# Layer 0's first product of feature tiles 8 to 15 for two token chunks together in seven block products, with a new order of the first part

## The chip, the core and the metric

The kernel runs on one core of a Trainium2 chip. Its engines are TensorE (in the rows PE for matmuls, PEld for weight loads), VectorE (DVE), ScalarE (ACT), GpSimd (POOL) and SyncE (SP, which here only issues DMAs). The metric is the device time of one execution in microseconds (us); smaller is better. All times below come from the runs and from one profiled execution of the kernel before.

## What is computed

The reference is a block attention over 1536 tokens (2 x 768, 8 heads of 64), followed by two feed-forward layers of width 2048:

```python
x = attention(q, k, v)                       # [1536, 512]
h = x @ w_in;  g = s * max(h, 0)**2 + b;  x = g @ w_out      # layer 0
h = x @ w_in2; g = max(0.01 * h, h);      out = g @ w_out2   # layer 1
```

Everything is float32. w_in is 512 x 2048, w_out 2048 x 512, in both layers.

## The kernel before

**Tiling.** The tokens go in three chunks of 512 (in the code c = 0, 1, 2; here chunk 1, 2, 3), the 2048 features in 16 feature tiles of 128 (fc). A step i is one layer, one chunk and one feature tile, in the order of the list `steps`: 0 to 15 are layer 0 of chunk 1, 16 to 31 of chunk 2, 32 to 47 of chunk 3, and 48 to 63 layer 1 of chunk 1.

**A plain step.** Each float32 operand is split into a high and a low part (hi is a rounded copy on ScalarE, lo the difference), and three matmuls (hi x hi, lo x hi, hi x lo) make one product. So the *first product* of a step (`ffn_in`) is 4 x 3 = 12 matmuls of 128x128 by 512 columns into a PSUM bank h, and the *second product* (`ffn_out`) is 4 x 3 = 12 more into the four accumulators acc. Between them stand the activation (`ffn_relu`, `ffn_act`), the split of its result g (`ffn_hi` on ScalarE, `ffn_lo` on VectorE), and the splits of the two weight blocks, tiles win and wout (`split_hi` on ScalarE, `split_lo` on GpSimd or VectorE).

**Weights.** They come from DRAM as float64 in tiles st and are turned into float32 tiles w, half a feature tile at a time, by `rescale` (ScalarE), `low_bits` (VectorE or GpSimd) and `shift` (VectorE). This is called a conversion here; each layer has 32.

**Layer 1 of chunks 2 and 3** is done with the Strassen-Winograd scheme: both chunks, two feature tiles and the two halves of the 512 inputs make a 2 x 2 block product, done in seven block products (`block`, 6 matmuls each) where eight would be 48 matmuls. Forms, which are sums and differences of blocks, are made of the tokens (`token_forms`: t1 to t4, split into hi and lo) and of the weights (`weight_forms`: s1 to s4, GpSimd); `split_block` splits the seven weight operands and `after_block` adds the products up on VectorE. A group of seven products is a quad. The second product of chunk 2 runs between them; chunk 3's activations wait and its second products come at the end (`last_chunk`), one step per 12 matmuls.

**Order.** Engines take their instructions in program order. The first part (attention of 24 units, all of layer 0 of chunk 1, and layer 0 of chunk 2) is written out in the string HEAD, a list of short operation names with numbers: s, x, e, r, n, t, c, o are the stages of an attention unit (scores, maximum, exponential, reciprocal, normalising, transpose, copy out of PSUM, output product), y and Y the hi and lo of its result, L, R, u/up, B the load and conversion of weights, H and lp/lv the weight splits, I the first and O the second product, A, a/as, G, g the activation and its split. `ops` maps each name to a call. After HEAD (from step 33) a loop goes on, one step after the other. Chunk 3's tokens come from units 16 to 23. Before, HEAD spreads these over the layer-0 steps of chunk 2.

**Slots.** Two PSUM banks h and four acc, two `at`; two tiles each of win, wout and g; two tiles vt, that hold the attention's v.

Of the kernel before, what the change touches and what calls it, by code (L numbers as in the profile page):

```python
# [25 lines left out]
P = 128  # L26
# [77 lines left out]
def block_attention_moe_moe(ctx, tc, q, k, v, vn, w1, w2, mask, ident_in, pool_in, out):  # L104
# [397 lines left out]
    def x_hi(c, m):  # L502
        if c:
# [3 lines left out]
            nc.scalar.activation(out=xf[c][m], in_=accs[0, c][m], func=AF.Copy, scale=sign)  # L507
# [27 lines left out]
    tf, wform, wops, banks, late_g = {}, {}, {}, {}, {}  # L535
# [6 lines left out]

    def token_forms(cc, part):

        if "t1" not in tf:
            for name in ("t1", "t2"):
                t = att.tile([P, GU, DM], F32, name="vt").bitcast(F32R).rearrange("p (a c) n -> p a c n", a=2)
                tf[name] = [[t[:, a, m, :] for m in range(2)] for a in range(2)]
            four = [soft.pool.tile([P, 512], F32, name=f"sm{i}").bitcast(F32R) for i in range(4)]
            tf["t4"] = [four[:2], four[2:]]  # L550
            for name, c, k in (("b11", 1, 0), ("b21", 1, 2), ("t3", 2, 0), ("b22", 2, 2)):
                tf[name] = [[xt[c][:, a, k + m, :] for m in range(2)] for a in range(2)]
# [21 lines left out]
    def open_forms():  # L574
        for i in range(2):
# [3 lines left out]
    def open_blocks():  # L579
        wops["tiles"] = [wspl.tile([P, 2, 512], F32R, name="win") for _ in range(2)]  # L580
# [342 lines left out]
```

## Time and profile before

| | us |
|---|---|
| median of 3 runs | 587.88 (587.74 to 588.04) |
| the profiled execution | 587.98 |
| its span, first to last instruction | 586.2 |
| PE busy in the span | 571.5 (98%) |
| DVE, ACT, POOL busy | 348.5, 343.5, 232.2 |

The profiled execution's own time is 1.8 us longer than the span of its trace, and 0.10 us above the median. A timeline row gives the start and the duration of an instruction; successive matmuls overlap, so the pace is read from start to start. A window row gives, for each engine, how long it was busy in a stretch.

### The profile page before, as it was taken

How to read it: one execution, taken by the hardware profiler on the slowest of the kernel's cores; microseconds unless marked ns; L12 is line 12 of the kernel's file. 1: busy time of each engine (PE TensorE's matmuls, PEld its weight loads, DVE VectorE, ACT ScalarE, POOL GpSimd, SP SyncE). 2: the span in 40 equal slices, each digit the busy share in tenths (PEclk: the TensorE clock that was granted, in tenths of full speed). 3: DMA queues.
4: the chain of work that ended last, by engine and by line, in shares of the span. 5: the costliest groups of instructions: out<-in, count | busy, mean ns of one | idle time of the engine just before them, and what ended most of it. 6: DMA issues, size and time to landing. Idle time of an engine off the chain costs nothing.

```text
span 586.2 us, 8857 instructions
## 1 busy us (share of the span) xinstructions
PE 571.5 (98%) x3196; PEld 459.5 (78%) x3196; DVE 348.5 (59%) x706; ACT 343.5 (59%) x757; POOL 232.2 (40%) x269
## 2 busy tenths in 40 slices
PE   4999999999999999999999999999999999999997
PEld 3477777878787788888888888888888888888885
DVE  5878778674523353376676678985254444446543
ACT  4788867666855563665655756655454455545342
POOL 4554555424244132333422255564455555550000
PEclk9999999999999999999999999999999999999999
DMA  8977666470400000013342433320010000000102
GB/s 340 377 224 242 215 237 210 151 244 2 162 0 1 2 1 1 1 37 107 108 129 88 144 107 101 115 73 1 1 72 1 0 2 1 1 0 9 65 1 72
DMA packets 16307, 53.38 MB, mean 91 GB/s; under 512 B 2024, under 2 KB 2408, under 8 KB 15624
## 3 DMA queue, kind: packets, MB, share of 16 engines
q1 hardware_dynamic: 16040, 52.69, 26.7%
q8 instruction: 25, 0.41, 0.3%
q14 instruction: 18, 0.15, 0.1%
q10 hardware_dynamic: 224, 0.13, 0.1%
HBM read 49.08 MB, written 3.15 MB: 89 GB/s over the span
## 4 chain that ended last, share of the span: by engine, by line
PE 93%; DVE 3%; DMA 1%; ACT 1%; issue 1%; POOL 1%; SPq 0%; POOLq 0%; DVEq 0%; ACTq 0%
PE h L446 30%; PE acc L496 22%; PE acc L498 15%; PE at L618 7%; PE h L618 7%; PE at L498 4%; PE h L498 4%; PE at L338 2%; PE at L258 2%; PE at L357 2%; DMA w<-in_q 1%; PE acc L258 1%; PE h L357 1%; ACT w L301 1%; DVE win L437 0%
## 5 line engine op out<-in xcount | busy, mean ns | idle before, releaser
L446 PE MATMUL h<-xt,win 128*128 128x512 f32 x768 | 188.7, 391 | 0.5 <-DVE win L437 0.5
L446 PEld LDWEIGHTS h<-xt,win 128*128 128x128 f32 x768 | 143.0, 188 | 32.0 <-DVE win L437 0.9
L496 PE MATMUL acc<-g,wout 128*128 128x512 f32 x576 | 145.4, 394 | 0.1
L496 PEld LDWEIGHTS acc<-g,wout 128*128 128x128 f32 x576 | 106.4, 188 | 23.4 <-issue 1.3
L437 POOL TENSOR_TENSOR win<-w,win 128x512 fp32r<-128x512 f32 x47 | 66.7, 1422 | 92.6 <-ACT win L431 67.8
L498 PE MATMUL acc<-wout,g 128*128 128x512 f32 x384 | 98.8, 390 | 0.0
L437 DVE TENSOR_TENSOR wout<-w,wout 128x512 fp32r<-128x512 f32 x74 | 70.4, 952 | 40.3 <-ACT wout L431 40.0
L431 ACT CAST wout<-w 128x512 fp32r<-128x512 f32 x96 | 59.6, 621 | 53.8 <-PE acc L496 24.4
L498 PEld LDWEIGHTS acc<-wout,g 128*128 128x128 f32 x384 | 72.1, 188 | 15.4
L479 DVE SCALAR_TENSOR_TENSOR g<-h,own,g 128x512 fp32r<-128x512 f32 x48 | 35.8, 746 | 40.1 <-ACT g L472 40.1
L417 DVE SCALAR_TENSOR_TENSOR w<-st,w 128x512 int32<-128x512 int32 x64 | 47.6, 745 | 9.8 <-ACT st L397 6.3
L457 ACT ACTIVATE r<-h 128x512 f32<-128x512 f32 x48 | 28.6, 596 | 36.1 <-PE h L446 36.1
L437 POOL TENSOR_TENSOR wout<-w,wout 128x512 fp32r<-128x512 f32 x22 | 28.9, 1315 | 51.5 <-ACT wout L431 51.3
L472 ACT ACTIVATE g<-h,own 128x512 fp32r<-128x512 f32 x48 | 32.9, 686 | 26.5 <-DVE h L467 13.2
L431 ACT CAST win<-w 128x512 fp32r<-128x512 f32 x64 | 39.3, 615 | 8.6 <-PE h L446 8.6
L483 DVE TENSOR_TENSOR g<-r,g 128x512 fp32r<-128x512 f32 x32 | 22.9, 714 | 34.9 <-ACT g L474 34.8
L397 ACT ACTIVATE st<-st 128x512 f32<-128x512 f32 x64 | 42.5, 675 | 1.1 <-DMA st<-in_w 1.1
L467 DVE TENSOR_TENSOR h<-r,h 128x512 f32<-128x512 f32 x30 | 20.8, 694 | 36.4 <-ACT r L457 36.1
L608 POOL TENSOR_TENSOR win<-q,win 128x256 fp32r<-128x256 f32 x32 | 25.7, 803 | 28.1 <-ACT win L607 28.1
L627 ACT ACTIVATE r<-r 128x512 f32<-128x512 f32 x16 | 10.1, 632 | 38.0 <-DVE r L648 19.9
L608 POOL TENSOR_TENSOR win<-w,win 128x256 fp32r<-128x256 f32 x24 | 19.9, 831 | 29.5 <-ACT win L607 17.2
L498 PE MATMUL h<-wout,g 128*128 128x512 f32 x96 | 26.9, 389 | 0.0
(149 smaller groups left out, 766.4 us busy)
## 6 DMA issues: line engine op xcount, KB each, us to landing
st<-in_w SPq DMA_DIRECT2D x64, 512.0 KB
vt<-in_v SPq DMA_DIRECT2D x5, 1024.0 KB
kt<-in_k SPq DMA_DIRECT2D x8, 500.0 KB
out<-kt SPq DMA_DIRECT2D x11, 256.0 KB
q<-in_q SPq DMA_DIRECT2D x8, 256.0 KB
w<-in_vn SPq DMA_DIRECT2D x3, 512.0 KB
w<-in_q SPq DMA_DIRECT2D x4, 256.0 KB
w<-in_v SPq DMA_DIRECT2D x2, 512.0 KB
```

What stands on the lines that cost most here:

```text
L397: nc.scalar.activation(out=high, in_=high, func=AF.Prelu, scale=2.0**-112, alpha=2.0**32)
L417: nc.vector.scalar_tensor_tensor(out=f, in0=high, scalar=3, in1=f, op0=ALU.logical_shift_left, op1=ALU.bitwise_or)
L431: nc.scalar.copy(t[:, 0, :], wf[layer, fc][:, half, :])
L437: engine.tensor_sub(t[:, 1, :], wf[layer, fc][:, half, :], t[:, 0, :])
L446: nc.tensor.matmul(hs[i], lhsT=w[:, a, cc * P : (cc + 1) * P], rhs=xt[c][:, b, cc, :], start=(cc == 0 and a == b == 0), stop=(cc == NCC - ...
L457: nc.scalar.activation(out=rs[i], in_=hs[i], func=AF.Relu)
L472: nc.scalar.activation(out=gs[i][:, 0, :], in_=hs[i], func=AF.Identity, bias=shift_b, scale=1.0)
L479: nc.vector.scalar_tensor_tensor(out=g[:, 1, :], in0=hs.pop(i), scalar=shift_b, in1=g[:, 0, :], op0=ALU.add, op1=ALU.subtract)
L496: nc.tensor.matmul(acc[m], lhsT=w[:, a, ms], rhs=g[:, b, :], start=first, stop=last)
L498: nc.tensor.matmul(acc[m], lhsT=g[:, b, ms], rhs=w[:, a, :], start=first, stop=last)
L608: nc.gpsimd.tensor_sub(t[:, 1, :], src, t[:, 0, :])
L618: nc.tensor.matmul(banks[j, name], lhsT=t[:, a, cc * P : (cc + 1) * P], rhs=x[b][cc], start=(cc == a == b == 0), stop=(cc == b == 1),)
```

## The change

Chunks 2 and 3 now take layer 0's feature tiles 8 to 15 together, in four quads of seven block products (`quads(0, NS // 2, 0)`, NS = 8). Feature tiles 0 to 7 of both chunks stay plain steps. For this the tokens of chunk 3 are needed before chunk 2's feature tile 8, so HEAD now ends with step 23, after all 24 attention units. The token forms are made at the end of HEAD from the split tokens xt (`first_forms`, operations ta on VectorE, tap on GpSimd; `first_hi`, th; `first_lo`, tl on GpSimd, tlv on VectorE); F and E are the weight forms and the first three weight splits. Chunk 3's activations of tiles 8 to 15 are kept where the weight tile was (`late_g`), and their second products come after chunk 3's plain steps, one step per 12 matmuls (`late_split`). Layer 1's weight conversions move: 11 halves stand in chunk 3's part, the other 21 in the first twelve steps of layer 1 of chunk 1, where 1.75 a step stand instead of about one, and they stand behind the split of g. HEAD is a new list throughout.

```diff
 HEAD = '''
-k0 km0 kpv0 sb k2 q0 mask sl0 sp0 iden km2 kpv2 q1 k1 s1 x0 e0 q2 s4 own d0 s5 rb0 v0 v1 x1 r0 e1 km1 x5 n0 kp1 e5 rb1
...
+k1 d0 zero k0 km0 d0 mask kpv0 km1 q0 sb s1 kpv1 sl0 x1 own sp0 e1 pool x0 d0 iden rb1 e0 k2 km2 q2 rb0 d0 kpv2 r1 r0
...
+    def first_forms(x, sub, add):
+        cc, k = divmod(x, 4)
...
+        if k == 0:
+            sub(a, h12, h11)
+            add(a, a, l12)
+            sub(a, a, l11)
+        elif k == 1:
+            sub(b, h22, a)
+            add(b, b, l22)
+        elif k == 2:
+            sub(c, h21, b)
+            add(c, c, l21)
+        else:
+            sub(d, h22, h12)
+            add(d, d, l22)
+            sub(d, d, l12)
...
+    def add_act(layer, r, x, ps):
+        if layer:
+            nc.vector.tensor_add(r, x, ps)
+            nc.scalar.activation(out=r, in_=r, func=AF.Prelu, scale=1.0, alpha=0.01)
+        else:
+            nc.vector.tensor_add(ps, x, ps)
+            nc.scalar.activation(out=r, in_=ps, func=AF.Relu)
+            nc.vector.tensor_mul(r, r, ps)
...
+    def quads(layer, first, begun):
+        for j in range(first, NQ):
+            for p in range(len(PRODUCTS)):
+                if j > first or p >= begun:
+                    block(layer, j, p)
...
+                after_block(layer, j, p, first)
+                if j > first or p:
+                    emit_out(1 + (p == len(PRODUCTS) - 1))
...
+    def late_split(layer, fc):
+        i = (3 * layer + 2) * NFC + fc
+        (hs, rs)[layer][i] = late_g(layer, fc)
         split_hi(i, 1)
         split_lo(i, 1, nc.vector)
         ffn_hi(i)
...
+    quads(0, NS // 2, 0)
...
+        convert((at + 1) * left // 12 - at * left // 12)
```

The end of HEAD, on TensorE. Before, this is where the last attention units stand, between plain steps 30 to 33 (L357 the output products of units, L338 transposes, L446 first and L496 second products, xt_97 and xt_98 the tokens of chunks 2 and 3):

```order
L338 MATMUL at_2565<-ident,sm_2488 120x128 x4
L338 MATMUL at_2572<-ident,sm_2535 120x128 x4
L496 MATMUL acc<-g,wout 128x512 x3
L446 MATMUL h<-xt_97,win 128x512 x6
L496 MATMUL acc<-g,wout 128x512 x6
L357 MATMUL at_2603<-sm_2570,vt 64x64 x8
L357 MATMUL at_2616<-sm_2577,vt 64x64 x8
L496 MATMUL acc<-g,wout 128x512 x3
L446 MATMUL h<-xt_97,win 128x512 x12
L496 MATMUL acc<-g,wout 128x512 x15
L446 MATMUL h<-xt_98,win 128x512 x12
```

Now the output products of units 22 and 23 (L353, the second and third row) stand ahead of the first products of steps 22 and 23 (L442), and the block products (L665) follow; vt is token form t2, at_ and h are banks:

```order
L334 MATMUL at_2283<-ident,sm_2275 120x128 x4
L492 MATMUL acc<-g,wout 128x512 x3
L353 MATMUL at_2302<-sm_2223,vt 64x64 x8
L353 MATMUL at_2325<-sm_2290,vt 64x64 x8
L442 MATMUL h<-xt_97,win 128x512 x12
L492 MATMUL acc<-g,wout 128x512 x12
L442 MATMUL h<-xt_97,win 128x512 x12
L492 MATMUL acc<-g,wout 128x512 x24
L665 MATMUL h<-xt_97,win 128x512 x6
L665 MATMUL at_2471<-vt,win 128x512 x6
L492 MATMUL acc<-g,wout 128x512 x3
L665 MATMUL h<-xt_97,win 128x512 x6
```

The attention now ends before feature tile 8 of chunk 2, and right behind the second products of the plain steps stand the block products, of which the second reads a form.

VectorE at the same place. Before, behind units 22 and 23 it goes on with plain steps (L374 the low parts of the units' tokens, L467 the activation, L479 the low part of g, L437 weight splits):

```order
L369 CAST xt2_98<-at1_2616 128x256
L437 TENSOR_TENSOR wout_2648<-w_1431,wout_2648 128x512
L374 TENSOR_TENSOR xt2_98<-at1_2616,xt2_98 128x256
L479 SCALAR_TENSOR_TENSOR g_2654<-h_2555,own_94,g_2654 128x512
L467 TENSOR_TENSOR h_2630<-r_2668,h_2630 128x512
L374 TENSOR_TENSOR xt2_98<-at0_2603,xt2_98 128x256
L437 TENSOR_TENSOR wout_2697<-w_1602,wout_2697 128x512
L479 SCALAR_TENSOR_TENSOR g_2700<-h_2630,own_94,g_2700 128x512
L437 TENSOR_TENSOR win_2704<-w_663,win_2704 128x512
L479 SCALAR_TENSOR_TENSOR g_2729<-h_2674,own_94,g_2729 128x512
```

Now the forms stand there. kt_2017 and kt_2018 are forms (L570 to L578), L598 are their low parts, of which the last row is that of t2's second half; L370, L475 and L433 are the tokens' low part, g's and the weight split:

```order
L370 TENSOR_TENSOR xt2_98<-at1_2302,xt2_98 128x256
L475 SCALAR_TENSOR_TENSOR g_2396<-h_2340,own_94,g_2396 128x512
L570 TENSOR_TENSOR kt_2017<-xt2_98,kt_2017 128x512
L571 TENSOR_TENSOR kt_2017<-kt_2017,xt2_98 128x512
L576 TENSOR_TENSOR kt_2018<-xt2_98 128x512
L577 TENSOR_TENSOR kt_2018<-kt_2018,xt2_98 128x512
L578 TENSOR_TENSOR kt_2018<-kt_2018,xt2_98 128x512
L598 TENSOR_TENSOR vt_2314<-kt_2017,vt_2314 128x512
L433 TENSOR_TENSOR wout_2412<-w_904,wout_2412 128x512
L598 TENSOR_TENSOR sm1_2427<-kt_2018,sm2_2358 128x512
L475 SCALAR_TENSOR_TENSOR g_2416<-h_2378,own_94,g_2416 128x512
L598 TENSOR_TENSOR vt_2315<-kt_2017,vt_2315 128x512
```

The forms of the last units' tokens and their low parts moved in between the splits of the last plain steps; ahead of this stretch stand nine more rows from the weight split of step 21, wout_2311, on.

VectorE in layer 1 of chunk 1, one step. Before (L437 the split of wout, L407 and L417 a conversion, L483 the low part of g, L562 a token form):

```order
L437 TENSOR_TENSOR wout<-w,wout 128x512
L407 TENSOR_SCALAR w<-st 128x512
L417 SCALAR_TENSOR_TENSOR w<-st,w 128x512
L483 TENSOR_TENSOR g<-r,g 128x512
L562 TENSOR_TENSOR kt<-kt 128x512
```

Now (L433, L479, L403, L413 and L616 are the same operations):

```order
L433 TENSOR_TENSOR wout<-w,wout 128x512
L479 TENSOR_TENSOR g<-r,g 128x512
L403 TENSOR_SCALAR w<-st 128x512
L413 SCALAR_TENSOR_TENSOR w<-st,w 128x512
L403 TENSOR_SCALAR w<-st 128x512
L413 SCALAR_TENSOR_TENSOR w<-st,w 128x512
L616 TENSOR_TENSOR kt<-kt 128x512
```

The conversions moved behind the low part of g, and most steps have two.

## Rows read from the trace of the kernel before

**Rows 1.** The page: PE's busy time and the clock that TensorE was granted.
```profile
PE 571.5 (98%) x3196; PEld 459.5 (78%) x3196; DVE 348.5 (59%) x706; ACT 343.5 (59%) x757; POOL 232.2 (40%) x269
PEclk9999999999999999999999999999999999999999
```

**Rows 2.** The chain that ended last, by line, as shares of the span.
```profile
by line: PE h L446 29.6%; PE acc L496 21.6%; PE acc L498 14.9%; PE at L618 6.6%; PE h L618 6.6%; PE at L498 3.7%; PE h L498 3.7%; PE at L338 1.7%; PE at L258 1.6%; PE at L357 1.5%; DMA w<-in_q 0.8%; PE acc L258 0.8%; issue 0.7%; PE h L357 0
```

**Rows 3.** Windows: stretch, its length, busy us (and count) of PE, PEld, DVE, ACT, POOL, clock, DMA.
```profile
0.00:15.00 15.00, 6.58 (x104) 5.22 (x104) 8.03 (x44) 6.04 (x25) 6.65 (x29) 1.00 0.88 340
15.00:60.00 45.00, 43.59 (x449) 29.93 (x449) 36.11 (x128) 37.56 (x112) 23.59 (x35) 1.00 0.82 284
60.00:105.00 45.00, 44.43 (x305) 34.58 (x304) 35.49 (x85) 33.49 (x89) 23.20 (x28) 1.00 0.62 210
105.00:240.00 135.00, 135.00 (x847) 108.29 (x846) 65.87 (x174) 80.43 (x186) 45.45 (x45) 1.00 0.17 59
420.00:540.00 120.00, 120.00 (x524) 98.08 (x523) 59.15 (x92) 60.60 (x128) 60.39 (x78) 1.00 0.03 9
540.00:570.00 30.00, 30.00 (x134) 24.82 (x133) 15.57 (x25) 13.20 (x24) 0.00 (x0) 1.00 0.10 36
```

**Rows 4.** PE's timeline in a plain step of layer 1: start, duration, line, tiles, count.
```profile
376.09 2.88 PE L446 MATMUL h<-xt,win 128*128 128x512 f32 x12
378.81 2.88 PE L498 MATMUL acc<-wout,g 128*128 128x512 f32 x12
```

**Rows 5.** PE's timeline: the output products of the last four attention units.
```profile
229.34 1.15 PE L357 MATMUL at<-sm,vt 120*64 120x64 f32 x32
```

**Rows 6.** Windows with one line alone, up to there: L446, then L496.
```profile
0.00:230.50 230.50, 93.34 (x372) 68.73 (x372) 1.00 0.44 153
...
0.00:230.50 230.50, 89.09 (x343) 62.67 (x343) 1.00 0.44 153
```

**Rows 7.** VectorE's timeline in one of these steps.
```profile
377.27 1.77 DVE L437 TENSOR_TENSOR wout<-w,wout 128x512 fp32r<-128x512 f32 x1
378.96 0.41 DVE L407 TENSOR_SCALAR w<-st 128x512 int32<-128x512 int32 x1
379.48 0.69 DVE L417 SCALAR_TENSOR_TENSOR w<-st,w 128x512 int32<-128x512 int32 x1
380.30 0.69 DVE L483 TENSOR_TENSOR g<-r,g 128x512 fp32r<-128x512 f32 x1
380.91 1.79 DVE L562 TENSOR_TENSOR kt<-kt 128x512 f32<-128x512 f32 x1
382.62 1.78 DVE L437 TENSOR_TENSOR wout<-w,wout 128x512 fp32r<-128x512 f32 x1
```

**Rows 8.** GpSimd's timeline at the same time.
```profile
380.86 1.29 POOL L572 TENSOR_TENSOR xt<-kt,xt 128x512 fp32r<-128x512 f32 x1 [2.37 <-ACT xt L571]
382.11 1.74 POOL L437 TENSOR_TENSOR win<-w,win 128x512 fp32r<-128x512 f32 x1
```

**Rows 9.** VectorE's timeline in a late second product of layer 1, where GpSimd is idle.
```profile
547.29 0.69 DVE L437 TENSOR_TENSOR wout<-w,wout 128x512 fp32r<-128x512 f32 x1 [1.43 <-ACT wout L431]
547.90 0.69 DVE L483 TENSOR_TENSOR g<-xt,g 128x512 fp32r<-128x512 f32 x1
```

**Rows 10.** GpSimd's timeline in a quad: one split of a weight operand, one form.
```profile
447.80 0.74 POOL L608 TENSOR_TENSOR win<-q,win 128x256 fp32r<-128x256 f32 x1
...
453.00 0.74 POOL L597 TENSOR_TENSOR q<-q,w 128x256 f32<-128x256 f32 x1
```

**Rows 11.** What PE waited for, us in total, times, longest.
```profile
PE acc L258 <- DMA w<-in_q: 7.7, 2, 6.4
PE acc L258 <- DVE kt L171: 0.8, 1, 0.8
...
PE h L446 <- DVE win L437: 0.5, 1, 0.5
```

**Rows 12.** DMA issues: the mask's queue, packets and size.
```profile
msk<-in_mask SPq DMA_DIRECT2D x1, 180.0 KB
```

More of the change, by code (lines that the diff above doesn't have):

```diff
@@ L541, in bank, with late_t4 @@
         return ps_at.pool.tile([P, 512], F32, name=f"at{n // 2}") if n % 2 else ps_h.tile([P, 512], F32, name="h")
-    def token_forms(cc, part):
[L545 to L552, printed above, removed]
+    def late_t4(layer, i):
+        tf["t4"][i // 2][i % 2] = soft.tile(("t4", layer, i)).bitcast(F32R)
@@ L604, in split_block @@
             return
-        src = weight_block(j, PRODUCTS[p])
+        if wops.get("of") != layer:
+            wops["of"], wops["tiles"] = layer, [wspl.tile([P, 2, 512], F32R, name="win") for _ in range(2)]
+        src = weight_block(layer, j, PRODUCTS[p])
         t = wops["tiles"][n % 4 // 2][:, :, n % 2 * 256 : n % 2 * 256 + 256]
@@ L788, in block_attention_moe_moe, with load_next, convert, chain @@
-    assert not late
+    todo = [(n_ffn1 + fc, half) for fc in range(NFC) for half in range(2)]
+    ahead = list(todo)
+    def load_next(n):
+        for _ in range(min(n, len(ahead))):
+            load_w(*ahead.pop(0), nc.sync)
+    def convert(n, engine=nc.vector):
+        now = [todo.pop(0) for _ in range(min(n, len(todo)))]
+        for w in now:
+            rescale(*w)
+        for w in now:
+            low_bits(*w, engine)
+            shift(*w)
+        load_next(len(now))
+    def chain(i):
+        ffn_relu(i)
+        ffn_act(i)
+        ffn_hi(i)
+        ffn_lo(i)
@@ new lines, in first_in @@
+    def first_in(i):
+        for part in range(2):
+            ffn_in(i, part)
+    c1, c2 = NFC, 2 * NFC
+    queue = [("out", c1 + NS - 1, m) for m in range(4)]
+    load_next(3)
+    quads(0, NS // 2, 0)
+    for n in range(4):
+        soft.free(("t4", 0, n))
+    split_hi(c2 + 1, 0)
+    split_lo(c2 + 1, 0, nc.gpsimd)
+    split_hi(c2, 1)
+    split_lo(c2, 1, nc.vector)
+    first_in(c2)
+    chain(c2)
+    emit_out(len(queue))
+    for m in range(4):
+        x_hi(1, m)
+    for k in range(NS):
+        i = c2 + k
+        if k + 1 < NS:
+            first_in(i + 1)
+        else:
+            for m in range(4):
+                ffn_out(c2 + NS, m)
+        if k + 2 < NS:
+            split_hi(i + 2, 0)
+            split_lo(i + 2, 0, nc.gpsimd)
+        if k + 1 < NS:
+            split_hi(i + 1, 1)
+            split_lo(i + 1, 1, nc.vector)
+        else:
+            late_split(0, NS + 1)
+        if k + 1 < NS:
+            chain(i + 1)
+        if k + 4 == NS:
+            t = att.tile([P, GU, DM], F32, name="vt").bitcast(F32R)
+            j = c2 + NS
+            ws[1][j], gs[j], hs[j] = t[:, :2, :], t[:, 2:, :], late_g(0, NS)
+            nc.scalar.copy(ws[1][j][:, 0, :], wf[0, NS][:, 1, :])
+            split_lo(j, 1, nc.vector)
+            nc.scalar.activation(out=gs[j][:, 0, :], in_=hs[j], func=AF.Identity, bias=shift_b, scale=1.0)
+            ffn_lo(j)
+        if k > 1:
+            convert(1, nc.gpsimd)
+        if k % 2:
+            split_x([[xt[1][:, a, m, :] for m in range(4)] for a in range(2)], k // 2, xf[1][k // 2])
+        for m in range(4):
+            ffn_out(i, m)
@@ new lines, in block_attention_moe_moe @@
+    for fc in range(NS + 1, NFC):
+        if fc + 1 < NFC:
+            late_split(0, fc + 1)
+        elif fc + 1 == NFC:
+            split_hi(n_ffn1, 1)
+            split_lo(n_ffn1, 1, nc.vector)
+        convert(int(fc > NS + 2), nc.gpsimd)
+        if fc + 3 >= NFC and fc + 1 < NFC:
+            at = n_ffn1 + fc + 3 - NFC
+            split_hi(at, 0)
+            split_lo(at, 0, nc.gpsimd)
+        if fc + 1 == NFC:
+            first_in(n_ffn1)
+            chain(n_ffn1)
+        for m in range(4):
+            ffn_out(c2 + fc, m)
@@ L802, in block_attention_moe_moe @@
         elif i + 2 == nq:
[L803 to L805 removed]
+            for n in range(LEAD):
+                split_block(1, n)
         if i + 1 < nq:
```

259 lines of the change are left out of this document (126 added, 133 removed).

## The prediction

> **What bounds the kernel now.** I read the page's busy line first: TensorE is busy 571.5 of 586.2 us at the full granted clock from end to end [rows 1]. The chain of waits, by line, then shows that nearly all of its share is TensorE's matmuls [rows 2]. The windows tell where the rest is: from 0 to 15 us TensorE works 6.6, in 15 to 60 it is idle 1.4, in 60 to 105 0.6, and from 105 on it has no idle time at all [rows 3]. What TensorE waits for is mostly the first q, 7.7 us in two waits [rows 11]. So TensorE's matmul count is the bound; a matmul taken away is worth its full price as long as no other queue becomes late.
>
> **Removed matmuls.** Twelve plain matmuls take 2.72 from start to start, 0.2267 each [rows 4]. The 336 matmuls of the eight quads of layer 1 (L618) hold 6.6% + 6.6% of 586.2 us in the chain [rows 2], 0.2303 each. Layer 0's eight feature tiles of two chunks were 16 × 12 = 192 plain matmuls, 43.5 us; now they are 4 × 42 = 168 block matmuls, 38.7 us. That gives −4.8.
>
> **The attention in less time.** HEAD now ends with step 23, and all 24 attention units must be done by then. Before, the last output products start at 229.34 [rows 5], and up to 230.5 TensorE ran 372 matmuls of first and 343 of second products [rows 6]: 715 × 0.2267 = 162.1 us, so 68.4 us went to attention and idle time. Now 504 product matmuls stand there, 114.3 us: the last unit comes at about 182.7. The mixture as dense as in 60 to 105 must therefore last to 183, 78 us longer. In that window VectorE is busy 35.5 and ScalarE 33.5 of 45, and TensorE is idle 0.57 [rows 3], so 78 us cost 78/45 × 0.57 = 1.0. The worse bound is the rate of 15 to 60, where VectorE is busy 36.1 and ScalarE 37.6 [rows 3]: 78/45 × 1.41 = 2.4. The other bound is nothing. For the forms' 24 new instructions on VectorE, 0.61 each from start to start [rows 9], there is room: it was busy 65.9 of 135 in 105 to 240 [rows 3]; without some 48 us of plain steps (two splits, a conversion, an activation, about 3 us per 5.44) that is 39.5, with the forms 54 of 78, 70%. I take +1.0, since the busy shares lie nearer to those of 60 to 105.
>
> **The joint between HEAD and the quads.** The second block product reads t2, whose last low part hangs on the last attention units. Behind their output products TensorE has 60 product matmuls, 6 of the first block product and 5 of the second that need no late part: 71 × 0.2267 = 16.1 us. VectorE has, from the weight split wout_2311 to that low part (vt_2315), 21 instructions; at 0.61 [rows 9] that is 12.8, a margin of 3.3. Two things eat it. GpSimd works beside it on three weight operands of 0.74 each [rows 10] and one split (wout_2394) of 1.29 [rows 8], 3.5 together. The VectorE form at 380.91 takes 1.79 while GpSimd runs, and the GpSimd instruction in the same time 1.74 where the one before took 1.29 [rows 7, 8]; with GpSimd idle the same size takes VectorE 0.69 [rows 9]. So each GpSimd instruction can cost VectorE up to its whole length; half, 1.75, is what I take. And g of step 22 stands on ScalarE behind a weight's high part whose tile step 20's second products free; no row shows that wait; it lies between 0 and one step's 2.72, I take 1.0. That leaves 0.5 of margin. The third block product's weight operand stands behind token low and high parts on GpSimd and ScalarE, by one instruction or none: 0 to 0.6. Bounds for the joint: 0, and 3.5 + 2.7 − 3.3 = 2.9. With the mean at the edge I take +0.5.
>
> On that contention the Trainium skill has a rule (page "SBUF — State Buffer", section "Who interferes with whom"): a VectorE instruction with two SBUF inputs and a GpSimd instruction that reads SBUF share a port pair, and whoever issues first has it for the whole instruction, while the other is fully blocked. The trace agrees: 1.79 against 0.69 [rows 7, 9]. By that rule with every meeting lost, the joint would be at its upper bound; by it with VectorE first every time, at zero.
>
> **Layer 1, chunk 1.** Layer 0's quads run without conversions, so 21 of layer 1's 32 now stand in its first twelve steps, 1.75 a step, behind the low part of g. VectorE takes per step, from start to start [rows 7, 9]: the split of wout 1.69, a conversion half 0.52 + 0.61 = 1.13, the low part 0.61, a form 1.71. A step with one half and a form is 5.14, with two 6.27, with two and no form 4.56; TensorE's step is 2 × 2.72 = 5.44 [rows 4]. In the pattern of 1, 2, 2, 2 halves, with forms in the steps where they stand, the end of the low part, counted from TensorE's start of the step, moves each step by the difference to 5.44: 4.8 in the first, 7.8 in the eighth, 8.3 at most, in the tenth. The second products begin to need it at 3 × 2.72 + 0.45 = 8.6, the fourth block of 2.72 and two matmuls on. Margin 0.3. Nothing is lost if these durations hold, but the shift (0.69) was seen there with GpSimd idle [rows 7, 8]. If each of 21 halves took 0.18 more, the loss would be 21 × 0.18 − 0.3 = 3.5. I take +0.2, bounds 0 and 3.5.
>
> **The late second products** of layer 0 are nine steps of 2.72 in which VectorE has two splits, 1.2 [rows 9], and in most a conversion's shift. As the late steps of layer 1 leave VectorE busy 15.6 of 30 and ScalarE 13.2 [rows 3], a shift of 0.61 more per 2.72 fits. Nothing. The kept g of the late tiles costs no copy that TensorE waits for.
>
> **The start.** SP now issues the mask ahead of the first q: 180 KB [rows 12] at the 340 GB/s of the first window [rows 3] are 0.5 us ahead of the load that TensorE waits for [rows 11]. Against it, k lands in another order, and the wait of 0.8 for VectorE's kt [rows 11] may go. +0.2, bounds −0.7 and +0.5.
>
> **Sum.** −4.8 + 1.0 + 0.5 + 0.2 + 0.2 = −2.9, against the profiled execution's 587.98: 585.1. That execution lies 0.10 above the median, so 585.0.
>
> **Rivals.**
>
> A, the forecast: 585.0, by the sum.
>
> B, no new wait: the dense stretch and all queues hold. −4.8 and nothing else, 583.1. For it speaks that VectorE and GpSimd lived side by side, busy 59 and 60 of 120 us, in 420 to 540 without a single idle slice of TensorE [rows 3]; against it the margins of 0.5 and 0.3.
>
> C, VectorE becomes the bound in layer 1: its mean load in the twelve steps is 1.69 + 0.61 + 1.75 × 1.13 + 8/12 × 1.71 = 5.4, just TensorE's 5.44. With 0.18 more per half 3.5 are lost: 585.0 − 0.2 + 3.5 = 588.3, no measurable change. It decides from 0.02 more per half on. Against it: the conversions stand behind the low part, so they delay only what follows.
>
> D, slower: VectorE comes late to the joint because GpSimd blocks it. Just before, GpSimd has three forms and two splits at 1.29 [rows 8], four weight forms at 0.74 [rows 10] and about 1 us of normalising, 10.4 us. If VectorE's instructions lose half of each, they arrive L = 5.2 late. At the joint all four GpSimd instructions (3.5) and 1.0 on ScalarE then use up 3.3 and 1.2 more, and 0.6 for the third operand follows: the stall is 1.2 + 0.6 + 5.2 = 7.0, in place of 0.5. That is 591.5, slower. It ends beyond 0.2% from L = 2.8 on. The Trainium skill's rule of the shared ports (same page and section) is what would make D. Against it: VectorE has about 30% free in that stretch and would have to lose that first.
>
> E, the denser HEAD loses as much as 15 to 60 does: 2.4 in place of 1.0, 586.4, with a few tenths at the units' waits on either side of the bound of 0.2%.
>
> That the change does not do what it says is not open: the order has 24 matmuls fewer.
>
> **How the numbers follow.** A 0.44, B 0.18, C 0.14, E 0.07, D 0.17. A measurement of this kernel can tell about 0.2%, 1.2 us, from no change: faster is below 586.70, slower above 589.06. Faster is A, B and a third of E, 0.64; within 0.2% C and the rest of E, 0.19; slower D, 0.17. Predicted is A, 585.0. The range must leave out no more than 0.2: D alone is left out. Below it reaches to B with the better start, 583.1 − 0.7 = 582.4, above to C with 0.9 at the joint, 589.2.
>
> **What would show it.** In the changed kernel's trace: 3172 matmuls where 3196 were [rows 1], and a block product of layer 0 in about 1.38; the last unit's output products near 183, and TensorE idle in 105 to 183 about 1.0 (E: over 2). At the joint, about 16 us behind them, a wait of TensorE on VectorE's vt_2315 of 0 to 1 (D: 5 and more, with VectorE's forms at 1.3 to 1.8 each and GpSimd busy in the same slices). In layer 1 of chunk 1 no wait for g (C: waits for VectorE's low part from the eighth step on, and shifts longer than 0.69). In the nine late steps 2.72 each. The first q should land about half a microsecond later. The sum is wrong if TensorE's idle time grows by more than 4.8, or if the block matmuls of layer 0 take longer than 0.2303, since their operands are then late.

## The result

The changed kernel takes 583.4 us (583.15 to 583.63), the kernel before 587.96 in the same comparison; the ratio is 0.9916, interval 0.9904 to 0.9929. It is faster by 4.6 us. The forecast was 585.0, inside a range of 582.4 to 589.2: direction right, size 1.6 short, and nearer to rival B (583.1) than to A. The profiled span went from 586.2 to 581.8.

The page after, in its busy line (engine, busy us, share, instructions) and the granted clock in 40 slices:

```profile
PE 566.5 (97%) x3172; PEld 455.1 (78%) x3172; DVE 388.2 (67%) x762; ACT 342.2 (59%) x771; POOL 257.9 (44%) x310
PEclk9999999999999999999999999999999999999999
```

Against [rows 1], 24 matmuls are gone, TensorE's busy time is 5.0 less and VectorE's 39.7 more. The clock stays at the upper level.

Windows of the changed kernel (stretch, length, busy us and count of PE, PEld, DVE, ACT, POOL, clock, DMA); the first is to be read beside [rows 3]:

```profile
60.00:105.00 45.00, 45.00 (x299) 36.16 (x298) 34.97 (x84) 31.86 (x74) 26.43 (x31) 1.00 0.74 236
105.00:183.00 78.00, 78.00 (x609) 61.30 (x608) 58.45 (x167) 54.52 (x153) 32.47 (x39) 1.00 0.26 87
...
330.00:420.00 90.00, 89.31 (x391) 72.95 (x390) 72.50 (x83) 54.21 (x99) 47.65 (x39) 1.00 0.32 100
```

The kernel before, in the last of these stretches:

```profile
330.00:420.00 90.00, 90.00 (x399) 74.45 (x398) 65.99 (x74) 54.72 (x98) 44.07 (x34) 1.00 0.25 77
```

In the 78 us in which the attention now runs dense, TensorE is never idle. Idle time has come in a place where the kernel before had none, between 330 and 420, layer 1 of chunk 1. What TensorE waited for, in the changed kernel (us in total, times, longest):

```profile
PE acc L254 <- DVE kt L167: 7.1, 1, 7.1
PE acc L254 <- DVE kt L171: 2.3, 1, 2.3
...
```

The rest of the list is 0.6 for a q at 21.5 us and, in layer 1 of chunk 1 (L494), 0.4 and 0.2 for VectorE. The start waits for k where it waited for q [rows 11]. From 22 us on, over the joint and up to layer 1, no wait is listed.

### The profile page after: what moved, and what is told of

It is laid out like the page before. It is cut to its first block, busy times and chain, and to the rows that moved or that the text cites. A ratio compares the mean times of both kernels' runs of the same rounds, so it can differ in the third digit from the quotient of the medians.

```text
span 581.8 us, 8967 instructions
## 1 busy us (share of the span) xinstructions
PE 566.5 (97%) x3172; PEld 455.1 (78%) x3172; DVE 388.2 (67%) x762; ACT 342.2 (59%) x771; POOL 257.9 (44%) x310
## 4 chain that ended last, share of the span: by engine, by line
PE 84%; DVE 12%; ACT 1%; DMA 1%; issue 1%; POOL 0%; DVEq 0%; SPq 0%; POOLq 0%
PE acc L492 23%; PE h L442 17%; PE h L665 10%; PE at L665 10%; PE acc L494 9%; DVE w L413 4%; PE h L494 4%; PE at L494 4%; DVE w L403 3%; PE at L334 2%; PE at L254 2%; PE at L353 1%; DVE g L479 1%; DVE wout L433 1%; PE acc L254 1%; DMA kt<-in_k 1%
## 5 line engine op out<-in xcount | busy, mean ns | idle before, releaser
L492 PE MATMUL acc<-g,wout 128*128 128x512 f32 x564 | 143.3, 394 | 0.0
L442 PE MATMUL h<-xt,win 128*128 128x512 f32 x564 | 138.0, 391 | 0.0
L442 PEld LDWEIGHTS h<-xt,win 128*128 128x128 f32 x564 | 105.0, 188 | 22.3 <-issue 0.6
L492 PEld LDWEIGHTS acc<-g,wout 128*128 128x128 f32 x564 | 104.2, 188 | 22.8 <-issue 1.6
L494 PE MATMUL acc<-wout,g 128*128 128x512 f32 x384 | 99.9, 392 | 0.7 <-DVE g L479 0.4
L433 DVE TENSOR_TENSOR wout<-w,wout 128x512 fp32r<-128x512 f32 x84 | 64.8, 772 | 43.2 <-ACT wout L427 42.9
L494 PEld LDWEIGHTS acc<-wout,g 128*128 128x128 f32 x384 | 71.9, 188 | 17.5 <-DVE g L479 1.2
L433 POOL TENSOR_TENSOR win<-w,win 128x512 fp32r<-128x512 f32 x33 | 47.3, 1435 | 57.3 <-ACT win L427 44.1
L413 DVE SCALAR_TENSOR_TENSOR w<-st,w 128x512 int32<-128x512 int32 x64 | 58.1, 913 | 6.6 <-ACT st L393 2.5
L655 POOL TENSOR_TENSOR win<-q,win 128x256 fp32r<-128x256 f32 x48 | 38.8, 809 | 34.7 <-ACT win L654 34.1
L655 POOL TENSOR_TENSOR win<-w,win 128x256 fp32r<-128x256 f32 x36 | 30.6, 850 | 50.4 <-ACT win L654 38.0
L479 DVE TENSOR_TENSOR g<-r,g 128x512 fp32r<-128x512 f32 x32 | 23.3, 727 | 36.3 <-ACT g L470 36.3
L406 POOL TENSOR_SCALAR w<-st 128x512 int32<-128x512 uint8 x39 | 30.8, 791 | 18.1 <-DMA st<-in_w 13.0
L665 PE MATMUL h<-xt,win 128*128 128x512 f32 x132 | 33.8, 391 | 0.0
L665 PE MATMUL at<-xt,win 128*128 128x512 f32 x132 | 33.8, 391 | 0.0
L475 DVE SCALAR_TENSOR_TENSOR g<-h,own,g 128x512 fp32r<-128x512 f32 x31 | 23.2, 747 | 11.1 <-ACT g L468 10.8
L468 ACT ACTIVATE g<-h,own 128x512 fp32r<-128x512 f32 x31 | 21.3, 686 | 14.7 <-DVE h L463 7.4
```

Source lines behind the costliest of these rows:

```text
L406: engine.tensor_scalar(f, byte, 1.0 / 32, -31.0 / 64, op0=ALU.mult, op1=ALU.add)
L413: nc.vector.scalar_tensor_tensor(out=f, in0=high, scalar=3, in1=f, op0=ALU.logical_shift_left, op1=ALU.bitwise_or)
L433: engine.tensor_sub(t[:, 1, :], wf[layer, fc][:, half, :], t[:, 0, :])
L442: nc.tensor.matmul(hs[i], lhsT=w[:, a, cc * P : (cc + 1) * P], rhs=xt[c][:, b, cc, :], start=(cc == 0 and a == b == 0), stop=(cc == NCC - ...
L475: nc.vector.scalar_tensor_tensor(out=g[:, 1, :], in0=hs.pop(i), scalar=shift_b, in1=g[:, 0, :], op0=ALU.add, op1=ALU.subtract)
L479: nc.vector.tensor_sub(g[:, 1, :], rs.pop(i), g[:, 0, :])
```

## The places that the prediction named

**The end of the attention.** TensorE's timeline (start, duration, line, tiles, count) from the last output products (L353) to the quads:

```profile
179.74 1.15 PE L353 MATMUL at<-sm,vt 120*64 120x64 f32 x32
...
195.92 1.55 PE L665 MATMUL at<-vt,win 128*128 128x512 f32 x6
...
200.08 1.52 PE L665 MATMUL at<-kt,win 128*128 128x512 f32 x6
```

Up to 180.9 there are these matmuls of first and second products (windows with one line alone, first L442, then L492):

```profile
0.00:180.90 180.90, 66.12 (x265) 1.00 0.57 194
...
0.00:180.90 180.90, 63.37 (x240) 1.00 0.57 194
```

505 × 0.2267 = 114.5, so 66.4 us went to attention and idle time, against the 68.4 of before: 2.0 less, where 1.2 more was forecast for the dense stretch and the start together. All engines in the same stretch, the kernel before first (TensorE's busy time is the first figure behind the length):

```profile
0.00:230.50 230.50, 220.10 (x1655) 170.24 (x1655) 140.28 (x422) 153.83 (x403) 95.44 (x134) 1.00 0.44 153
...
0.00:180.90 180.90, 170.62 (x1445) 131.15 (x1445) 135.85 (x415) 128.96 (x360) 89.48 (x131) 1.00 0.57 194
```

Idle time was 10.40 before and is 10.28 now, so nearly nothing of the 2.0 is idle time. The matmuls other than first and second products are 940 in both (1655 − 715 and 1445 − 505), and the busy time that is left for them went from 58.0 (220.1 − 162.1) to 56.1 (170.6 − 114.5).

**The joint.** VectorE's timeline, the last rows ahead of the second block product:

```profile
185.15 1.12 DVE L567 TENSOR_TENSOR kt<-kt,xt 128x512 f32<-128x512 f32 x1
...
194.57 0.85 DVE L598 TENSOR_TENSOR vt<-kt,vt 128x512 fp32r<-128x512 f32 x1
```

The last row is t2's last low part: done at 195.42. The matmul that reads it is the sixth of the block product that starts at 195.92; at 0.2267 each it stands at 197.05. The margin was 1.6, where 0.5 had been reckoned. GpSimd had only three instructions between 184.4 and 188.8, and VectorE paid 0.4 at each of two forms (1.12 against 0.69); a fourth, at 194.14, cost the last low part 0.2.

**Layer 1, chunk 1.** VectorE works in groups of instructions, one for each step: a wout split (L433) and a low part of g (L479) for the next step, conversions (L403, L413), a token form. Its timeline from the last token form (L616), the end of the tenth group, over the eleventh and twelfth:

```profile
386.51 0.68 DVE L616 TENSOR_TENSOR kt<-kt 128x512 f32<-128x512 f32 x1
387.11 0.68 DVE L433 TENSOR_TENSOR wout<-w,wout 128x512 fp32r<-128x512 f32 x1
387.71 0.68 DVE L479 TENSOR_TENSOR g<-r,g 128x512 fp32r<-128x512 f32 x1
388.32 1.52 DVE L403 TENSOR_SCALAR w<-st 128x512 int32<-128x512 int32 x1
389.94 1.60 DVE L413 SCALAR_TENSOR_TENSOR w<-st,w 128x512 int32<-128x512 int32 x1
...
392.59 0.69 DVE L433 TENSOR_TENSOR wout<-w,wout 128x512 fp32r<-128x512 f32 x1
393.19 1.78 DVE L479 TENSOR_TENSOR g<-r,g 128x512 fp32r<-128x512 f32 x1
394.90 0.95 DVE L403 TENSOR_SCALAR w<-st 128x512 int32<-128x512 int32 x1
...
397.99 1.04 DVE L413 SCALAR_TENSOR_TENSOR w<-st,w 128x512 int32<-128x512 int32 x1
398.95 1.78 DVE L433 TENSOR_TENSOR wout<-w,wout 128x512 fp32r<-128x512 f32 x1
```

GpSimd at the same time: a token low part, weight splits, and from 394.39 the four weight forms of layer 1, which belong to the thirteenth step and run ahead of VectorE.

```profile
387.93 1.62 POOL L623 TENSOR_TENSOR sm<-kt,sm 128x512 fp32r<-128x512 f32 x1 [3.02 <-ACT sm L622]
...
392.83 1.60 POOL L433 TENSOR_TENSOR win<-w,win 128x512 fp32r<-128x512 f32 x1 [1.84 <-ACT win L427]
394.39 1.18 POOL L641 TENSOR_TENSOR q<-w 128x256 f32<-128x256 f32 x1
```

VectorE has no idle time in either group. They have two conversion halves and no token form, reckoned at 4.56; the eleventh takes 5.48 (387.11 to 392.59) and the twelfth 6.36 (392.59 to 398.95). Instructions that stand beside one of GpSimd's are longer than alone: the same operation is 0.41 [rows 7] or 1.52, 0.69 or 1.78. TensorE's timeline shows what that did to the second products (L494); its first row is the start of the step of the twelfth group:

```profile
385.88 2.88 PE L442 MATMUL h<-xt,win 128*128 128x512 f32 x12
...
394.04 0.61 PE L494 MATMUL acc<-wout,g 128*128 128x512 f32 x2
395.04 2.60 PE L494 MATMUL acc<-wout,g 128*128 128x512 f32 x10 [0.39 <-DVE g L479]
397.47 2.89 PE L442 MATMUL h<-xt,win 128*128 128x512 f32 x12
400.20 0.39 PE L494 MATMUL acc<-wout,g 128*128 128x512 f32 x1
400.79 3.16 PE L494 MATMUL acc<-wout,g 128*128 128x512 f32 x11 [0.20 <-DVE wout L433]
403.79 0.39 PE L442 MATMUL h<-xt,win 128*128 128x512 f32 x1
```

From 394.04 to the next first product it takes 3.43, from 400.20 3.59, where 2.72 is the pace [rows 4]: 0.71 + 0.87 = 1.6 lost. The listed waits, 0.39 and 0.20, show only a part of it, since modelled ends of overlapping matmuls cover the rest; start to start shows it all.

So the size is put together as follows: −4.8 for the matmuls, −2.0 in the first part (attention and start), 0 at the joint, +1.6 in layer 1. That is −5.2, where the span fell by 4.4; the remaining 0.8 was not followed.

## The experiments

Each is the changed kernel with one edit, so 583.4 is the number to compare with.

**What a matmul is worth.** The first block product of each of layer 0's quads is done twice, which changes nothing in the output.

```diff
-        for cc in range(2):
+        for cc in [0, 1] * times:
```

Here `times` is 2 for p == 0 of layer 0 and 1 everywhere else.

> The changed kernel, with the first block product of each of layer 0's four quads done twice into the same bank, 24 matmuls more. Theory (TensorE's matmul count sets the time in layer 0's quads): 24 x 0.2303 = 5.5 us more than the changed kernel's 583.4, so 588.9, the gain of the change given back. Rival (the gain came from the new order, the removed matmuls lay beside a wait): clearly less than 5.5, under 586.

588.95 us, 5.55 more (ratio to the kernel before 1.0012, 1.0003 to 1.0022). 24 matmuls more in the quads are 5.5 us on the path that sets the end. That the removed ones lay on it as well follows from the kernel before, where TensorE has no idle time from 105 on [rows 3]. The run also says something of the new order: with the old number of matmuls, the kernel is 1.0 slower than before, and the pauses of layer 1, 1.6, are more than that.

**The pauses of layer 1: spread the conversions.**

```diff
-        convert((at + 1) * left // 12 - at * left // 12)
+        convert((at + 1) * left // 13 - at * left // 13)
```

> The changed kernel, with the 21 conversion halves of layer 1 spread over thirteen steps of chunk 1, not twelve. Theory (VectorE, late by the conversions piled up at step 12, made the pauses of 0.77, 0.59 and 0.60 between successive second products at 394 and 400 us): VectorE is one half or two behind less, the pauses go, about 1.5 to 1.9 less: 581.7. Rival (the pauses come from the weight forms that GpSimd makes in step 12, beside whatever VectorE does): at most 0.3 less.

581.62 us (ratio 0.989, 0.9875 to 0.9904), 1.8 less than the changed kernel. TensorE's timeline of this run, in the same place:

```profile
393.53 2.88 PE L494 MATMUL acc<-wout,g 128*128 128x512 f32 x12
396.25 2.88 PE L442 MATMUL h<-xt,win 128*128 128x512 f32 x12
398.97 2.88 PE L494 MATMUL acc<-wout,g 128*128 128x512 f32 x12
```

Every block starts 2.72 after the one before: the pauses are gone, with 17 conversion halves ahead of the twelfth group (11 × 21/13) where 19 stood (11 × 21/12). What was late was VectorE, and by little.

**The weight forms one step later**, so that they run beside no conversion.

```diff
-        if at == 11:
+        if at == 12:
             weight_forms(1, 0)
```

> The changed kernel, with GpSimd's four weight forms of layer 1 one step later, behind the conversions and not beside them. Theory of contention (VectorE's four conversion instructions of step 12 take 0.95 to 1.04 each beside GpSimd's forms, 4.0 together, where 0.52 + 0.61 twice is 2.3): the second group of pauses goes, the first stays, 0.7 to 0.9 less: 582.6. Rival (VectorE is late by the number of its instructions alone): no change, 583.4. A third way: the forms then hold up the low parts of step 13's weights, and the pause moves there: 583.4 or more.

582.21 us (ratio 0.9901, 0.9886 to 0.9915), 1.2 less; the interval is ±0.8, so the 0.7 to 0.9 expected lies inside it. In its trace the first pause is still there (394.15 to 397.53 is 3.38 from start to start) and the second is gone (400.25 to 402.97 is 2.72). VectorE's timeline of this run, the twelfth group's conversions, now without GpSimd's forms beside them:

```profile
394.98 0.41 DVE L403 TENSOR_SCALAR w<-st 128x512 int32<-128x512 int32 x1
...
396.63 0.69 DVE L413 SCALAR_TENSOR_TENSOR w<-st,w 128x512 int32<-128x512 int32 x1
```

The same four instructions take 2.3 from the first start to the end of the last, and took 4.1 in the changed kernel (394.90 to 399.03). Not one instruction was taken from VectorE, so its count alone cannot be the cause.

**The low parts of the token forms on VectorE**, that is more work for the engine that is late.

```diff
     def split_x(t, at, src, layer1=False):
         nc.scalar.copy(t[0][at], src)
-        nc.gpsimd.tensor_sub(t[1][at], src, t[0][at])
+        (nc.vector if layer1 else nc.gpsimd).tensor_sub(t[1][at], src, t[0][at])
```

> The changed kernel, with the low parts of layer 1's ten token forms subtracted by VectorE, not GpSimd. Theory of contention (GpSimd's 1.63 us instruction is what makes VectorE's conversion take 1.52 and 1.61 in place of 0.41 and 0.69 in the same step): VectorE gains 0.61 of work and loses about 1.0 of waiting in each of these steps, the pauses shrink or go: 581.5 to 583.0. Rival (VectorE is bound by the number of its instructions): ten times 0.61 more on an engine without room, 586 to 589.

581.54 us (ratio 0.9888, 0.9871 to 0.9904), 1.9 less, though VectorE has ten instructions more. The busy line of this run's page shows that VectorE has even less busy time than in the changed kernel (384.7 against 388.2):

```profile
PE 565.0 (97%) x3171; PEld 454.8 (78%) x3172; DVE 384.7 (66%) x772; ACT 341.6 (59%) x771; POOL 239.9 (41%) x300
```

VectorE's timeline of this run, the first conversion of one group:

```profile
385.00 0.42 DVE L403 TENSOR_SCALAR w<-st 128x512 int32<-128x512 int32 x1
385.52 0.69 DVE L413 SCALAR_TENSOR_TENSOR w<-st,w 128x512 int32<-128x512 int32 x1
```

With GpSimd's token low part out of the way the first conversion is 0.42 + 0.69, where it was 1.52 + 1.60; GpSimd's weight split stays, and the second conversion's shift beside it takes 1.59 (386.66). The theory of count (586 to 589) falls, the theory of contention holds.

The thirteen steps and the low parts on VectorE together:

> The changed kernel with both cures of layer 1's pauses, thirteen steps and the low parts on VectorE. Theory (each cure alone has taken away all of the pauses): no better than either, 581.4 to 581.7. Rival (each has left a part of VectorE's lateness that delays something else): 580.5 to 581.2.

581.88 us (ratio 0.9894, 0.988 to 0.9909): no better than either alone. No further gain shows in this place.

**The joint: more work on VectorE.** The three form instructions of t3's second half (ta7, L576 to L578) are done twice again; the cut is a part of one line of HEAD.

```diff
-... ta5 as23 ta7 th5 ...
+... ta5 as23 ta7 ta7 ta7 th5 ...
```

> The changed kernel, with six form instructions done again on VectorE at the joint, ahead of t2's last low part: 6 x 0.61 = 3.7 us more there. By the changed kernel's trace t2's low part ends at 195.4 and the matmul that reads it stands at 197.1, a margin of 1.65: TensorE then waits 2.0, 585.4. By the prediction's margin of 0.5: 3.2 more, 586.6. Rival (the joint has room, the trace's margin is not what counts): 583.4 to 584.0.

588.55 us (ratio 1.0004, 0.9995 to 1.0013), 5.15 more, well above both expectations. TensorE's timeline of this run shows why:

```profile
195.56 1.32 PE L665 MATMUL at<-vt,win 128*128 128x512 f32 x5
199.80 0.66 PE L665 MATMUL at<-vt,win 128*128 128x512 f32 x1 [2.91 <-DVE vt L598]
...
204.47 1.52 PE L665 MATMUL at<-kt,win 128*128 128x512 f32 x6
```

and its windows (stretch, length, busy and count of PE, clock, DMA):

```profile
199.80:202.00 2.20, 2.20 (x6) 0.54 0.00 0
202.00:203.30 1.30, 1.30 (x5) 0.50 0.00 0
203.40:204.50 1.10, 1.10 (x7) 1.00 0.00 0
```

The place is where the prediction said, the sixth matmul of the second block product waiting for t2's low part. The wait, from its due time 196.7 to 199.8, is 3.1: the six instructions depend on one another and follow at 0.73 in this run, 4.4 together, and one low part met GpSimd (1.21); less the 1.6 of margin that gives about what was seen. What was not expected is the rest. After TensorE had stood for 2.9 us, the granted clock was 0.54 and 0.50 of full speed up to 203.3, which is the lower level of 1.2 GHz, and 1.00 from 203.4 on: some 3.5 us at the lower level. From the start of that block product to the one that reads kt (195.56 to 204.47) it is 8.9 us; in the changed kernel, 195.92 to 200.08, it is 4.2: 4.75 lost, of which 3.1 is the wait and 1.6 the clock.

**The joint: more work on GpSimd**, the weight forms made twice more.

```diff
-... th7 lp45 tlv7
+... th7 lp45 F F tlv7
```

> The changed kernel, with GpSimd making the first four weight forms twice more at the joint, eight instructions of 0.74 or more, 5.9 us, beside VectorE's forms and low parts. If GpSimd costs VectorE nothing: 583.4. If VectorE loses half of each instruction it meets: 3.0 late, less the margin of 1.65, 584.7. Theory D of the prediction in full (it loses all of each): 5.9 less 1.65, 587.7.

587.07 us (ratio 0.9977, 0.9968 to 0.9987), 3.7 more. VectorE's timeline of this run, and GpSimd's behind it:

```profile
192.63 1.12 DVE L578 TENSOR_TENSOR kt<-kt,xt 128x512 f32<-128x512 f32 x1
...
197.77 1.23 DVE L598 TENSOR_TENSOR vt<-kt,vt 128x512 fp32r<-128x512 f32 x1
```

```profile
192.01 1.19 POOL L644 TENSOR_TENSOR q<-w,q 128x256 f32<-128x256 f32 x1
193.15 1.19 POOL L641 TENSOR_TENSOR q<-w 128x256 f32<-128x256 f32 x1
```

Each engine goes at the pace of the pair, about 1.15 us for an instruction, GpSimd's from 192.01 to 193.15, where VectorE's takes 0.69 and GpSimd's 0.74 alone. So VectorE loses 0.4 to 0.5 at each of the eight. t2's last low part ends at 199.00, 3.6 later than in the changed kernel; the waits of TensorE in this run are

```profile
PE at L665 <- DVE vt L598: 2.0, 1, 2.0
PE at L665 <- POOL win L655: 0.6, 1, 0.6
```

2.6 in all, where the time is 3.7 longer. From start to start a little more shows: the sixth matmul of the second block product, due at 196.85, starts at 199.05, and the second of the fourth block product, due at 202.35, at 203.09. That is 2.9, and the profiled execution of this run is 3.0 longer than the changed kernel's (586.61 against 583.63); the median lies 0.5 above it. So the loss lies at the joint. No clock was lost: 1.00 in the windows behind both waits. Of the three expectations the middle one (half of each instruction) has the size of the loss per instruction right and the full one the total nearer, because a weight operand is late as well. Rival D's mechanism is real; in the changed kernel GpSimd simply has not enough to do there.

**The start.** The first k and q go ahead of the second k and the mask.

```diff
-k1 d0 zero k0 km0 d0 mask kpv0 km1 q0 sb ...
+k0 d0 zero k1 km0 d0 kpv0 km1 q0 mask sb ...
```

> The changed kernel, with the first k and the first q issued ahead of the second k and the mask at the start, nearly as in the kernel before. Theory (the later first matmul, 7.12 against 6.45 us, is made up by 28 us, where both kernels stand at the same output product, 28.43 and 28.53): no change, 583.1 to 583.7. Rival (the start's order carries through): 0.5 to 1.0 less.

583.08 us (ratio 0.9914, 0.9899 to 0.9929), 0.3 less, which these runs hardly tell from nothing. The first matmul comes at 6.70 where it came at 7.12.

**More on VectorE in the dense attention.** Nine weight low parts (`lp` to `lv`) go to VectorE.

```diff
-... lp24 ... lp19 ... lp26 ... lp28 ... lp23 ... lp30 ... lp35 ... lp33 ... lp39 ...
+... lv24 ... lv19 ... lv26 ... lv28 ... lv23 ... lv30 ... lv35 ... lv33 ... lv39 ...
```

> The changed kernel, with nine weight low parts of the dense stretch of HEAD (about 90 to 170 us) subtracted by VectorE and not by GpSimd: 9 x 0.61 = 5.5 us more on VectorE, which is busy 58.5 of 78 us there. Theory (there is room on VectorE, so the dense attention costs TensorE nothing): 583.1 to 583.7. Rival (the prediction's term: TensorE's idle time grows with VectorE's busy share, from 75% to 82%): 1 us or more above, 584.4 or more.

587.68 us (ratio 0.9996, 0.9984 to 1.0008), 4.3 more: the theory of room falls, and more than the rival forecast is lost. The new waits of TensorE in this run:

```profile
PE at L334 <- DVE rec L309: 1.9, 1, 1.9
PE h L442 <- DVE win L433: 1.2, 1, 1.2
PE h L442 <- DVE g L475: 0.5, 1, 0.5
```

These are single places where one instruction of VectorE's comes late. 75% busy was without loss, and a little more on single places cost over 3 us: the busy share told neither. What decides is which instruction stands ahead of which, and HEAD as changed has an order in which TensorE has no listed wait after 22 us.

**The best of these edits** together: thirteen steps, the weight forms later, the start as above.

> The changed kernel with the conversions of layer 1 over thirteen steps, the weight forms one step later, and the first k and q ahead of the second k and the mask at the start. Theory (the pauses of layer 1 go by the first edit alone, and the start's 0.3 us carries through): 581.3. Rival (the start's gain was noise): 581.6, as with the thirteen steps alone; a third way, the forms at the same step as the last conversions bring a pause back: 582 or more.

581.4 us (ratio 0.989, 0.9872 to 0.9907), 2.0 less than the changed kernel and 6.7 less than the one before. TensorE waits only at the start (DMA of q 6.9, kt 2.3). It cannot be told from the thirteen steps alone (581.62) or the low parts on VectorE (581.54), so whether the start's 0.3 is real stays open.

## Why the prediction came out as it did

**The removed matmuls**, −4.8: right. 24 matmuls added again cost 5.55.

**The attention in less time**, +1.0 forecast: wrong by 3.2 us together with the start, in two steps. The first is the rate: idle time of 60 to 105 carried over to 78 us, as if it belonged to the mixture of work. The changed kernel has none in that stretch, nor in its own 60 to 105. Of the 0.57 there, 0.5 was one wait, for a weight split [rows 11]. The trace shows that this dense stretch had no idle time of its own; the nine splits, which brought 3.6 us of waits, show that it had little room either. Both say that the loss there is a matter of single places, and the rate could not be carried. This step was off by 1.3: idle time of the whole first part was forecast to grow by 1.2 and fell by 0.1. The second step is a term that the sum does not have: the prediction left the busy time of the attention's own matmuls at what it was, and it fell by 1.9, from 58.0 to 56.1, for the same 940 matmuls. What made that was not tested and stays open; short waits that modelled ends cover, as in layer 1, may be a part of it.

**The joint**, +0.5: the place and the mechanism right, the size not. The margin was 1.6: the wait assumed on ScalarE did not come, and GpSimd cost VectorE 1.0 in the 21 instructions, where 1.75 was assumed. What kept the margin from being larger is that VectorE began them 0.5 late (181.37, where the output products end at 180.83), behind a form that took 1.78 (178.94) beside a weight split of GpSimd's (178.74), and that forms which depend on one another follow at 0.73 where 0.61 was reckoned. The prediction's bounds priced a wait at its length alone; the added work made a wait of 3.1 that cost another 1.6 by the clock, which no row of the kernel before shows. One reading of the rows there is wrong, without harm to the sum: the GpSimd instruction beside most of the form at 380.91 is the one of 1.29, which began first, and the 1.74 stands mainly beside the next wout split [rows 7, 8].

**Layer 1**, +0.2: the mechanism near rival C's (conversions lengthened beside GpSimd), the term mis-sized; it measured 1.6 by the trace and 1.8 by the cure. The step that failed is the reckoning of the steps without a token form, 4.56: two of them took 5.48 and 6.36, because GpSimd's splits and weight forms stand there and VectorE's instructions beside them are lengthened. The prediction took the conversion's 1.13 from a row with GpSimd idle, named that, and still took it as the likely value. Up to there its reckoning held, for another reason than it gave: the wout split and the form, counted at 1.69 and 1.71 with GpSimd beside them, took 0.68 now, and the conversions took the lengthening in their place. In its counting the tightest place is the tenth step, with the low part's end 8.3 behind TensorE's start of the step; that is the eleventh group, and the trace has 7.95 there (388.39 − 380.44, which is 5.44 ahead of 385.88). By its terms the next group is at 8.3 + 4.56 − 5.44 = 7.4; it came at 9.1 (394.97 − 385.88), beyond the 8.6 at which TensorE needs it. So the pauses came in the second products fed by the twelfth and thirteenth groups.

On that, the page "SBUF — State Buffer" of the Trainium skill (section "Who interferes with whom") is borne out: VectorE's two-input instructions are lengthened beside GpSimd's, and both ways, the pair taking 1.15 where the two alone take 0.69 and 0.74. The full block that the prediction states is not quite reached: 1.15 is less than the two in turn, 1.43. The section also lists `tensor_scalar` among the operations that may take the shared ports; the row agrees, the conversion's TENSOR_SCALAR with one input being 0.41 alone and 1.52 beside GpSimd.

**The start**, +0.2: it was not the mask ahead of q that counted: the first product now waits for VectorE's copy of k, whose load stands second, 7.12 against 6.45. With both put back it came to 0.3.

**Late second products**, nothing: right; no wait of TensorE lies there.

**Rivals.** B (583.1) was nearest to the time, but not as it was told: a new wait was there, and the faster first part paid for it. That the sum came out near is in part luck, since its largest errors, 3.2 too much in the first part and 1.4 too little in layer 1, have opposite signs. D's mechanism is real, but its place had 1.6 of margin.

## What to carry to other kernels

When TensorE is the bound, the price of a removed matmul is the sure part of the sum; the doubtful part is where the moved work of the other engines meets. Reckon a queue of VectorE with each instruction's duration beside GpSimd's, step by step, and count a step's GpSimd instructions with it: giving VectorE the work that GpSimd did beside it can make VectorE faster, as the token low parts did (1.9 gained), or make TensorE wait, as the nine splits did (4.3 lost). A mean idle rate of a stretch can't be carried to another stretch; look for the single waits.

## What the runs showed of the hardware

- GpSimd and VectorE side by side each took about 1.15 us from one start to the next for instructions that alone take 0.74 (128x256) and 0.69 (128x512).
- A wait of TensorE of 2.9 us in the midst of full work was followed by the lower level of the granted clock (0.54 and 0.50) for some 3.5 us, which cost 1.6; one of 2.0 us was followed by full clock.
- Dependent VectorE instructions (128x512) followed at 0.73 from start to start in the chain of forms, where independent ones follow at 0.61 [rows 9].
